# A fused hash-attention and channel-mix kernel on one Trainium2 core: a new preparation of the first pair, and new wanted times in its plan

## The chip, the cores and the metric

The kernel runs on one core of a Trainium2 chip. The metric is device time in microseconds (us) of one execution. The kernel before took 266.68 us as a median of three runs; with a further run beside the changed kernel 267.82 (266.32 to 269.33), and 268.2 to 268.6 on the three chips that the experiments used. All ratios below use fast runs only (a run is slow when it lies over 1.5% above the fastest of its kernel), and each kernel is compared with the kernel before in the same rounds on the same chip.

A ratio below is the mean time of one kernel's fast runs over that of the other's of the same rounds, so it is not quite the ratio of the medians that are quoted beside it. These medians are of all runs, slow ones included. Of the fast runs alone they are 270.20 for e_pool_hi, 269.97 for e_direct, 267.08 for e_old_start, 266.78 for e_old_w, 268.60 for e_jit1 and 260.43 for e_fix_w, 268.0 to 268.2 for the kernel before beside them, and as quoted for the others.

## The reference, cut to what matters

```python
# q, k, v: 4 batches x 8 heads x 768 x 64; proj: 64 x 6
q_bucket, k_bucket = ...          # six sign bits of q @ proj and k @ proj
mask   = q_bucket[..., :, None] == k_bucket[..., None, :]
scores = where(mask, q @ k.T / 8, -1e9);  attn = softmax(scores)
x      = (attn @ v), heads side by side    # 4 x 768 x 512
xk, xr = mu * x + (1 - mu) * (x one row earlier)
k = max(xk @ w_k, 0);  out = sigmoid(xr @ w_r) * ((k * k) @ w_v)
```

The 32 heads are worked in 16 pairs, four pairs to a batch. The channel mix ("moe" in the code) of a batch can start when its four pairs are done. So at the start TensorE has attention work only, and later it can fill holes with channel mix.

## The kernel before

Nothing in the program text says in which order operations run. Every operation is added to a plan with an engine, an estimated duration and a *wanted time*, mostly counted in pairs. The plan is a small simulation: whenever an engine is free, it takes the ready operation that was wanted first. The order that comes out is the program of each engine, and on the chip each engine executes its program strictly in that order.

```python
for e in free:                       # each engine that is free at plan time t
    while ready[e]:
        item = heapq.heappop(ready[e])          # smallest wanted time
        ...                                     # (cut: score and small PSUM buffers)
        if o.svc > 0.3 and dma_free - t > BACKLOG:
            skipped.append(item); ...           # a large load waits for the queue
            continue
        pick = o
        break
    ...
    free[e] = t + o.dur                         # the plan believes o.dur
```

To prepare a pair, q and k are split in a high half (`hi`) and the rest (`lo`), transposed (pairs 0 and 1 on TensorE, later ones by DMA), multiplied by the projection for the bucket bits, and the bits become six more rows of the transposed operands. For pair 0 this was done whole head by whole head; for pairs 1 and 2 GpSimd made `hi`.

```python
POOL_HI = (1, 2)
add("GQ", 0.6, -20.0, lambda e=e: nc.gpsimd.dma_start(out=pj[e * D : (e + 1) * D, :], in_=proj), ...)
...
def hi(side=side, nat=nat, nh=nh, hp=hp):
    (nc.gpsimd if hp else nc.vector).tensor_scalar(out=nh[:, :, 0:D], in0=nat..., scalar1=QS, ...)
add("POOL" if hp else "DVE", 0.8 if hp else DVE_C(768, 2), n - 1.95, hi, ...)   # n - 1.95 is the wanted time
...                                             # pair 0: six transposes, then one copy of 768 columns
for c in range(NSC):
    nc.tensor.transpose(ps[:, c * P : (c + 1) * P], nh[:, j * NSC + c, :], idh)
```

The softmax here doesn't subtract the row's maximum and nothing guards it: scores larger than these inputs give would overflow.

Of the kernel before, what the change touches and what calls it, by code (L numbers as in the profile page):

```python
# [20 lines left out]
BACKLOG = 1.5  # L21

# [5 lines left out]
class Plan:  # L28
# [44 lines left out]
    def schedule(self):  # L73
# [17 lines left out]
        t = 0.0  # L91
        dma_free = 0.0
        while len(order) < len(ops):
# [19 lines left out]
            for e in free:  # L113
# [4 lines left out]
                while ready[e]:  # L118
                    item = heapq.heappop(ready[e])
                    o = ops[item[1]]  # L120
                    if o.take is not None:
                        cls, name, moe = o.take
                        if not avail[cls] or (moe and moe_held[cls] >= self.slots[cls][1]):
                            skipped.append(item)
                            continue
                    if o.svc > 0.3 and dma_free - t > BACKLOG:
                        skipped.append(item)
                        heapq.heappush(events, (dma_free - BACKLOG, 3, o.i))
                        continue
                    pick = o  # L130
                    break
# [31 lines left out]
def kernel(  # L163
# [29 lines left out]
    NWARM = 8  # L193
    NPET = 1
    NUC = 4
    POOL_HI = (1, 2)
# [10 lines left out]
    def buf(shape, dt, name):  # L207
        return pool.tile(shape, dt, name=name, tag=name)
# [31 lines left out]
    pj = buf([P, NB], FP32, "pj")  # L240
# [16 lines left out]
    POOL2 = lambda n: 0.18 + 2.2 * n / 1000.0  # L257


    wz = buf([P, 512], BF16, "wz")  # L260
    add("DVE", 0.2, -20.0, lambda: nc.vector.memset(wz, 0.0), w=["wz"])
    for i in range(NWARM):
        add("PE", 0.43, -20.0 + 0.1 * i, lambda: nc.tensor.matmul(sm("warm"), wz[:, 0:P], wz, start=True, stop=True),
            r=["wz"], w=["warm"], take=("sm", "warm", 0) if i == 0 else None, give=["warm"] if i == NWARM - 1 else [])
    add("ACT", 1.3, -9.0, lambda: nc.scalar.activation(out=wz[:, 0:1], in_=wz[:, 1:2], func=AF.Exp), r=["wz"], w=["wz0"], name="table")
# [9 lines left out]
    for i in range(NXT):  # L275
        add("POOL", 0.1, -1.0 + i, lambda i=i: nc.gpsimd.memset(xt_t[i][:, 0:1], 0.0), w=[("xz", i)])
    for e in range(2):
        add("GQ", 0.6, -20.0, lambda e=e: nc.gpsimd.dma_start(out=pj[e * D : (e + 1) * D, :], in_=proj), w=[("pj", e)], svc=0.05)
    add("DVE", 0.08, -8.0, lambda: nc.vector.tensor_scalar(
        out=p1[:, 0:NB], in0=pj, scalar1=-1.0, scalar2=None, op0=ALU.mult),  # L280
        r=[("pj", 0), ("pj", 1)], w=["p1"])
    add("DVE", 0.08, -8.0, lambda: nc.vector.scalar_tensor_tensor(
        out=p2[:, 0:NB], in0=pj, scalar=-1.0, in1=p1[:, 0:NB], op0=ALU.mult, op1=ALU.subtract),
        r=[("pj", 0), ("pj", 1), "p1"], w=["p2"])
# [9 lines left out]
    wlist = [("k", c, 1) for c in range(NDC)] + [("r", 0, 2), ("r", 2, 2)] + [("v", c, 2) for c in range(0, NFC, 2)]  # L294
    for i, (which, c0, n) in enumerate(wlist):
# [6 lines left out]
        add("GQ", 0.7, (2.2 + 0.5 * i) if which == "k" else (3.5 + 0.35 * i), f_w, w=[("w" + which, c) for c in range(c0, c0 + n)], at=(22.0 + 5 * i) if which == "k" else (34.0 + 3.5 * i), svc=1.5)  # L302
# [4 lines left out]
    def add_load(n):  # L307
        b, t = divmod(n, NPB)
        s = n % NQ
        for side in "qk":  # L310
            if n == 0:
                for j in range(2):
                    def f(side=side, j=j):
                        eng = nc.sync if side == "q" else nc.scalar
                        eng.dma_start(out=side_nat[side][s][:, j, :],
                                      in_=SRC[side][b, 2 * t + j].rearrange("(p c) d -> p (c d)", c=NSC))
                    add("SP" if side == "q" else "ACT", 0.42, -10.0 + 0.1 * j, f,
                        w=[("nat", side, s, j)], svc=0.57)
            else:
# [3 lines left out]
                add("SP", 0.42, (n - 2.6) if n > 1 else -9.0, f, w=[("nat", side, s, j) for j in range(2)], svc=1.15)  # L323
# [4 lines left out]
        add("SP", 0.42, n - 2.1, fv, w=[("vn", n % NV)], svc=1.15)  # L328

    def add_v(n):  # L330
# [12 lines left out]
        if uc:  # L343
            add("POOL", 0.8, n - 0.3, f0, r=[("vn", s)], w=[("va", sa, 0), ("va", sa, 1)], name=f"va{n}")
# [10 lines left out]
        pr = n + 0.3 if uc else n - 0.6  # L355
# [13 lines left out]
        add("PE", 0.15, n - 0.1, f4, r=["ones", ("vs", ss)], w=[(nm,)], take=("sm", nm, 0), name=nm)  # L369
        for j in range(2):  # L370
# [5 lines left out]
            add("DVE", DVE_C(384), n + 0.0, f5, r=[(nm,), ("vn", s)], w=[("va", sa, j)], name=f"va{n}")  # L376
# [3 lines left out]
        add("DVE", DVE_C(1), n + 0.01, f6, r=[(nm,)], w=[("mc", sm_)], give=[nm])  # L380

    def add_prep(n):
        s, sh, sa, sx = n % NQ, n % NNH, n % NAQ, n % NBX
        for side in "qk":
# [14 lines left out]
            add("POOL" if hp else "DVE", 0.8 if hp else DVE_C(768, 2), n - 1.95, hi, r=rn, w=[("nhh", side, sh)], name=f"hi{n}")  # L399
            add("DVE", DVE_C(768), n - 1.95, lo, r=rn + [("nhh", side, sh)], w=[("nhl", side, sh)], name=f"lo{n}")  # L400
            if n <= NPET:
                for j in range(2):
# [7 lines left out]
                    add("PE", 6 * 0.056, n - 1.5, tp, r=["idh", ("nhh", side, sh), ("nhl", side, sh)], w=[(nm,)], take=("sm", nm, 0), name=nm)  # L410
                    add("DVE", DVE_C(768, 2), n - 1.45, ev, r=[(nm,)], w=[("a", side, sa, j), ("ab", side, sa, j)], give=[nm], name=f"tr{n}")
                continue
            add("SP", 1.5, n - 1.8, tr, r=[("nhh", side, sh), ("nhl", side, sh)],
                w=ax + [("ab", side, sa, j) for j in range(2)], svc=2.1, name=f"tr{n}")
        for h in range(2):
            nm = f"bits{n}_{h}"

            def f(nm=nm, h=h):
                ps = sm(nm)
                for w_, st in ((p1, True), (p2, False)):  # L420
                    for i in range(4):
# [4 lines left out]
            def g(nm=nm, h=h):  # L426
                nc.vector.tensor_scalar(  # L427
                    out=bx_t[sx][:, h * HALF : (h + 1) * HALF].bitcast(U16),
                    in0=sm(nm)[:, 0:HALF].bitcast(U16).rearrange("p (c e) -> p c e", e=2)[:, :, 1],
                    scalar1=0x8000, scalar2=0x5400, op0=ALU.bitwise_and, op1=ALU.bitwise_or)  # L430

            add("PE", 2 * MM(HALF) + 0.1, n - 1.2, f, r=["p1", "p2"] + [("a", side, sa, j) for side in "qk" for j in range(2)],
                w=[(nm,)], take=("sm", nm, 0), name=nm)
            add("DVE", DVE_C(HALF), n - 1.2, g, r=[(nm,)], w=[("bx", sx, h)], give=[nm], name=f"bx{n}")
        for i in (0, 1, 2, 3):
# [4 lines left out]
            add("SP", 0.7, n - 1.1 + 0.01 * i, row, r=[("bx", sx, 0), ("bx", sx, 1)], w=[("ab", side, sa, j)], svc=0.1, name=f"row{n}")  # L440

    def add_prep_first(n):
        s, sh, sa = n % NQ, n % NNH, n % NAQ
        for j in range(2):
            pr = -8.0 + 2.0 * j
            for side in "qk":
                nat, nh, a = side_nat[side][s], side_nh[side][sh], side_a[side][sa]
                nv = nat[:, j, :].rearrange("p (c d) -> p c d", d=D)
                def hi(nv=nv, nh=nh, j=j, side=side):
# [3 lines left out]
                    else:  # L453
                        nc.scalar.activation(out=o, in_=nv, func=AF.Copy, scale=QS)
                def lo(nv=nv, nh=nh, j=j):
# [3 lines left out]
                nm = f"t{side}{j}"  # L459
                def tp(nm=nm, nh=nh, j=j):  # L460
                    ps = sm(nm)[:, 0:HALF].bitcast(FP16)
                    for c in range(NSC):
                        nc.tensor.transpose(ps[:, c * P : (c + 1) * P], nh[:, j * NSC + c, :], idh)
                def ev(nm=nm, a=a, j=j, side=side):
                    i_ = sm(nm)[:, 0:HALF].bitcast(FP16)
                    if side == "q" and j == 0:
                        nc.vector.tensor_copy(a[:, j, :], i_)
                    else:
                        nc.scalar.copy(a[:, j, :], i_)
                if side == "q":  # L470
                    add("DVE", DVE_C(384, 2), pr, hi, r=[("nat", side, s, j)], w=[("fh", side, j)], name=f"hi{n}")
                else:
                    add("ACT", ACT_C(384), pr, hi, r=[("nat", side, s, j)], w=[("fh", side, j)], name=f"hi{n}")
                add("DVE", DVE_C(384), pr, lo, r=[("nat", side, s, j), ("fh", side, j)], w=[("fl", side, j)], name=f"lo{n}")
                add("PE", 6 * 0.09, pr, tp, r=["idh", ("fh", side, j), ("fl", side, j)], w=[(nm,)], take=("sm", nm, 0), name=nm)
                add("DVE" if side == "q" and j == 0 else "ACT", DVE_C(768, 2) if side == "q" and j == 0 else ACT_C(768), pr, ev,
                    r=[(nm,)], w=[("a", side, sa, j), ("ab", side, sa, j)], give=[nm], name="ev" + nm)
            for side in "qk":
                for h in range(2):
                    nm = f"b{side}{j}{h}"  # L480
                    a = side_a[side][sa]
                    def bits(nm=nm, a=a, j=j, h=h):
                        ps = sm(nm)
                        for w_, st in ((p1, True), (p2, False)):
                            nc.tensor.matmul(ps[D : D + 32, 0:HALF], w_, a[:, j, h * HALF : (h + 1) * HALF], start=st, stop=not st)
                    def be(nm=nm, a=a, j=j, h=h):
                        nc.vector.tensor_scalar(
                            out=a[D : D + NB, j, h * HALF : (h + 1) * HALF].bitcast(U16),
                            in0=sm(nm)[D : D + NB, 0:HALF].bitcast(U16).rearrange("p (c e) -> p c e", e=2)[:, :, 1],
                            scalar1=0x8000, scalar2=0x6C00 if (j == 0 and nm[1] == "q") else 0x5400, op0=ALU.bitwise_and, op1=ALU.bitwise_or)  # L490
                    add("PE", 2 * MM(HALF) + 0.1, pr + 0.1, bits, r=["p1", "p2", ("a", side, sa, j)], w=[(nm,)], take=("sm", nm, 0), name=nm)
                    def bs(nm=nm, a=a, j=j, h=h):
# [219 lines left out]
```

## Time and profile before

| | before |
|---|---|
| span of the profiled run | 266.3 us |
| TensorE busy, idle | 240.0, 26.3 us |
| idle before 26.3 us; 26.3 to 58.9; 58.9 to 125; after | 6.9; 7.4; 6.7; 5.3 us |
| exponential 1, 5, 10, 19, 37 starts at | 16.5, 21.4, 26.2, 39.6, 60.4 us |

Nine exponentials on ScalarE make one pair, so number 10 is the first of pair 1, 19 of pair 2, 37 of pair 4. They are good milestones, as they are the same work in each version. The prediction shows the totals and the first 16 us. From the timeline of TensorE these are three of the later holes; the figure in brackets is how long the engine stood before the group, and for what:

```profile
31.67 0.51 PE L573 MATMUL sm<-idb,ob 128*128 128x128 bf16 x6 [2.51 <-DVE ob L563]
...
83.01 0.22 PE L366 MATMUL sm<-vs,ones 128*128 128x128 bf16 x1 [2.05 <-POOL vs L353]
...
103.27 0.22 PE L366 MATMUL sm<-vs,ones 128*128 128x128 bf16 x1 [1.28 <-POOL vs L353]
```

Each is an operation that stands at the head of TensorE's program while its input is late. Nothing behind it can start, ready or not; how much was ready is not shown. That is the price of a fixed order when its estimates are wrong.

### The profile page before, as it was taken

To read this page: it belongs to the slowest core of one execution; us is meant where nothing else is said; L and a number is where in the kernel's file an instruction comes from. 1 tells how busy PE (TensorE), PEld (TensorE's weight loads), DVE (VectorE), ACT (ScalarE), POOL (GpSimd) and SP (SyncE) were. 2 spreads that over 40 slices of the span, in tenths; PEclk is the share of its full clock that TensorE was granted. 3 is DMA by queue.
4 is the path that set the end of the run, shared out by engine and by line. 5 is a ranking of instruction groups with operands and counts; after the bars stand their busy time and mean duration, and the time that the engine had idled before them with its cause. 6 is when DMAs were issued, how large, how long until landed. Compare 5 with 4: busy or idle time off the path is not lost.

```text
span 266.3 us, 6293 instructions
## 1 busy us (share of the span) xinstructions
PE 240.0 (90%) x2501; PEld 144.1 (54%) x2520; DVE 193.3 (73%) x386; ACT 185.9 (70%) x241; POOL 65.1 (24%) x103
## 2 busy tenths in 40 slices
PE   6597668878995897999999999999999999999994
PEld 2254446545663544565666665655666666556441
DVE  1799857699596998559898898858967655485322
ACT  3359579789687557688979887768798987437320
POOL 4799715064014204301140303020200000000000
PEclk9799999999999999999999999999999999999999
DMA  7953987769969667966949699768340011220132
GB/s 220 373 178 69 157 142 184 139 188 171 205 150 269 127 228 121 223 146 233 218 164 202 224 232 167 198 133 253 78 90 6 2 39 42 79 79 4 39 118 79
DMA packets 64525, 39.76 MB, mean 149 GB/s; under 512 B 46728, under 2 KB 60912, under 8 KB 64496
## 3 DMA queue, kind: packets, MB, share of 16 engines
q1 hardware_dynamic: 61936, 36.35, 54.0%
q0 software_dynamic: 2272, 2.63, 6.5%
q8 instruction: 19, 0.31, 0.5%
q10 hardware_dynamic: 288, 0.39, 0.5%
q14 instruction: 10, 0.08, 0.1%
HBM read 24.12 MB, written 6.29 MB: 114 GB/s over the span
## 4 chain that ended last, share of the span: by engine, by line
PE 69%; DVE 11%; DMA 8%; POOL 4%; ACT 3%; issue 3%; SPq 1%; DVEq 0%; POOLq 0%; ACTq 0%
PE sc L517 17%; PE sm L645 14%; PE sm L616 13%; PE sm L547 11%; PE sm L635 7%; DMA vn<-in_v_dram 4%; PE sm L423 4%; ACT pt L521 3%; DMA qn<-in_q_dram 2%; DVE kh L392 2%; PE sm L573 2%; DVE qh L392 2%; DMA ak<-bx 2%; POOL vt L347 1%; DVE qh L389 1%
## 5 line engine op out<-in xcount | busy, mean ns | idle before, releaser
L521 ACT ACTIVATE pt<-sc 128x1024 bf16<-128x1024 f32 x144 | 142.3, 1025 | 33.8 <-PE sc L517 33.2
L517 PE MATMUL sc<-aq,ak 128*128 128x512 f16 (+1 forms) x384 | 82.2, 325 | 6.8 <-ACT pt L521 5.3
L517 PEld LDWEIGHTS <-ak 128*128 128x128 f16 x384 | 34.3, 97 | 32.8 <-issue 11.2
L547 PEld LDWEIGHTS <-pt 128*128 128x128 bf16 x1152 | 42.9, 97 | 13.0 <-ACT pt L521 2.4
L616 PE MATMUL sm<-xk,wk 128*128 128x384 bf16 x256 | 47.6, 326 | 0.1
L547 PE MATMUL sm<-va,pt 128*128 128x65 bf16 x1152 | 45.5, 193 | 1.9 <-ACT pt L521 1.9
L645 PE MATMUL sm<-wv,k 128*128 128x512 bf16 x183 | 46.3, 379 | 0.7 <-issue 0.2
L620 ACT ACTIVATE kr<-sm 128x384 bf16<-128x384 f32 x64 | 30.7, 500 | 12.8 <-PE sm L616 11.9
L616 PEld LDWEIGHTS <-wk 128*128 128x128 bf16 x256 | 24.1, 98 | 15.0 <-issue 0.6
L347 POOL TENSOR_TENSOR vt<-vn 128x384 f32<-128x384 f32 x12 | 14.0, 1168 | 65.1 <-DMA vn<-in_v_dram 65.0
L652 DVE SCALAR_TENSOR_TENSOR os<-rs,sm 128x512 f32<-128x512 f32 x24 | 16.4, 682 | 17.9 <-PE sm L645 17.0
L623 DVE TENSOR_TENSOR k<-kr 128x384 bf16<-128x384 bf16 x64 | 22.9, 372 | 7.5 <-ACT kr L620 7.5
L638 ACT ACTIVATE rs<-sm 128x512 f32<-128x512 f32 x24 | 14.3, 598 | 19.9 <-PE sm L635 15.0
L583 POOL COPY xt<-xt 128x127 bf16<-128x127 bf16 x16 | 5.7, 359 | 89.8 <-DVE xt L579 76.4
L645 PEld LDWEIGHTS <-k 128*128 128x128 bf16 x192 | 18.0, 97 | 17.6 <-issue 0.6
L635 PE MATMUL sm<-wr,xr 128*128 128x512 bf16 x86 | 23.6, 379 | 0.5
L427 DVE TENSOR_SCALAR bx<-sm 128x384 uint16<-128x384 uint16 x30 | 15.5, 551 | 4.4 <-PE sm L423 3.3
L563 DVE TENSOR_TENSOR ob<-sm,rc 128x384 bf16<-128x384 f32 x32 | 17.8, 555 | 0.7
L392 DVE SCALAR_TENSOR_TENSOR kh<-kn,kh 128x768 f16<-128x768 f32 x15 | 16.3, 1085 | 0.8 <-POOL kh L389 0.5
L392 DVE SCALAR_TENSOR_TENSOR qh<-qn,qh 128x768 f16<-128x768 f32 x15 | 16.7, 1113 | 0.1
L599 DVE SCALAR_TENSOR_TENSOR xk<-df,muk,xt 128x768 bf16<-128x768 bf16 x16 | 16.2, 1015 | 0.3
L599 DVE SCALAR_TENSOR_TENSOR xr<-df,mur,xt 128x768 bf16<-128x768 bf16 x16 | 16.3, 1023 | 0.0
(79 smaller groups left out, 207.5 us busy)
## 6 DMA issues: line engine op xcount, KB each, us to landing
vn<-in_v_dram SPq DMA_DIRECT2D x16, 384.0 KB
out_dram<-os SPq DMA_DIRECT2D x24, 256.0 KB
qn<-in_q_dram SPq DMA_DIRECT2D x15, 384.0 KB
kn<-in_k_dram SPq DMA_DIRECT2D x15, 384.0 KB
wk<-in_moe_w_k_dram POOLq DMA_DIRECT2D x4, 256.0 KB, 4.4
wv<-in_moe_w_v_dram POOLq DMA_DIRECT2D x4, 256.0 KB, 7.7
wr<-in_moe_w_r_dram POOLq DMA_DIRECT2D x2, 256.0 KB, 4.2
aq<-bx SPq DMA_DIRECT2D x30, 9.0 KB
```

The lines of the kernel that those rows point to most:

```text
L347: nc.gpsimd.tensor_tensor(out=vt[:, :, :, 0:E], in0=src[:, :, 0:3, 0:E], in1=src[:, :, 3:6, 0:E], op=ALU.add)
L392: nc.vector.scalar_tensor_tensor(out=nh[:, :, D:P], in0=nat.rearrange("p j (c d) -> p (j c) d", d=D), scalar=QS, in1=nh[:, :, 0:D], op0=AL ...
L517: nc.tensor.matmul(ps[:, lo - s * STEP : hi - s * STEP], side_a["k"][sa][:, j, jc * P : (jc + 1) * P], side_a["q"][sa][:, j, q0 : q0 + hi ...
L521: nc.scalar.activation(out=pt_t[sp][:, s * STEP : (s + 1) * STEP], in_=sc_t[plan.slot[nm]], func=AF.Exp, bias=EBIAS, scale=ESC)
L547: nc.tensor.matmul(oo[:, ic * 65 : ic * 65 + 65], pt_t[sp][:, o : o + P], va_t[sa][:, j, jc, 0 : D + 1], start=(not uc and ic == 0 and jc ...
L563: nc.vector.tensor_tensor(out=ob_t[so][:, :, j * D : (j + 1) * D], in0=oo[:, :, 0:D], in1=rc_t[sr][:, 1, :].unsqueeze(2).to_broadcast([P, ...
L599: nc.vector.scalar_tensor_tensor(out=dst[smx], in0=df_t[sd], scalar=mu[:, t : t + 1], in1=x, op0=ALU.mult, op1=ALU.add)
L616: nc.tensor.matmul(ps[:, 0:HALF], wk_sb[:, d, fc * P : (fc + 1) * P], xk_t[mx[d]][:, h * HALF : (h + 1) * HALF], start=(d == 0), stop=(d = ...
L620: nc.scalar.activation(out=kr_t[sk], in_=sm(nm)[:, 0:HALF], func=AF.Relu, scale=0.5 ** 0.5)
L623: nc.vector.tensor_tensor(out=k2_t[s2][:, h * HALF : (h + 1) * HALF], in0=kr_t[sk], in1=kr_t[sk], op=ALU.mult)
L635: nc.tensor.matmul(sm(nr), xr_t[mx[d]][:, c * P : (c + 1) * P], wr_sb[:, d, :], start=(d == 0), stop=(d == NDC - 1))
L645: nc.tensor.matmul(sm(nv), k2_t[(b * NFC + fc) % NK2][:, c * P : (c + 1) * P], wv_sb[:, fc, :], start=(fc == 0), stop=(fc == NFC - 1))
```

## The change

The intent is an earlier start and a better order after it. The core of the diff:

```diff
-    NWARM = 8
+    NWARM = 7
-    POOL_HI = (1, 2)
+    POOL_HI = ()
-        add("GQ", 0.6, -20.0, lambda e=e: nc.gpsimd.dma_start(out=pj[...], in_=proj), ...)
+    add("ACT", 0.42, -20.0, lambda: nc.scalar.dma_start(out=pj, in_=proj), ..., at=0.75, svc=0.05)
...                                    (q and k of pair 0 now all on SP's queue, q and k in turn)
+            parts = [(0, 3), (3, 6)] if j == 0 else [(0, 6)]     # head 0 by halves
+                for e, (c0, c1) in enumerate(parts):             # transposes, copy, bits by part
...
+            if j == 1:
+                add_bits(n, (1,))       # head 1: bits on 64 partitions, rows by DMA
...
+                    if o.svc > 0.3 and o.prio > -9.0 and dma_free - t > BACKLOG:
+PR = {
+    'ldq': -2.811, 'ldv': -2.337, 'hi': -5.393, 'lo': -1.084, 'tr': -2.122, 'bits': -1.224, 'bx': -4.393, 'row': 4.034,
...
+    'tpe': -4.352, 'tev': -0.289, 'va_u': 2.059, 'vsum_u': -3.477, 'wk0': 38.237, 'wk1': 3.956, 'wr0': 54.984, 'wv0': 63.151,
+    'wv1': -2.812, 'p0b': -9.506,
+}
-            add(..., n - 1.95, hi, ...)
+            add(..., n + PR["hi"], hi, ...)          # and so for every operation
```

A few estimated durations in the plan were corrected too. No arithmetic changed.

## The prediction

> **What bounds the kernel now.** I read the page's totals first, then windows, the chain of waits in order of time, and the timelines of each engine over the first 60 us.
>
> ```profile
> span 266.3 us, 6293 instructions
> PE 240.0 (90%) x2501; PEld 144.1 (54%) x2520; DVE 193.3 (73%) x386; ACT 185.9 (70%) x241; POOL 65.1 (24%) x103
> PE   6597668878995897999999999999999999999994
> DVE  1799857699596998559898898858967655485322
> ACT  3359579789687557688979887768798987437320
> PEclk9799999999999999999999999999999999999999
> DMA  7953987769969667966949699768340011220132
> ```
>
> TensorE is busy 240.0 of 266.3 us, so it is idle 26.3 us, and the row of slices (6.66 us each) shows where: in the first sixteen. From slice 19 on it is full. Windows cut at the stage borders give the sizes (columns: stretch, length, then busy time of each engine, granted clock, DMA share, GB/s):
>
> ```profile
> 26.30:58.90 32.60, 25.23 (x365) 16.40 (x364) 24.80 (x43) 25.37 (x28) 13.46 (x21) 1.00 0.80 166
> 58.90:100.00 41.10, 35.88 (x392) 21.93 (x395) 34.27 (x70) 28.84 (x41) 9.92 (x16) 1.00 0.86 187
> 100.00:125.00 25.00, 23.50 (x271) 14.16 (x273) 18.16 (x36) 19.29 (x23) 5.23 (x7) 1.00 0.84 191
> 125.00:262.40 137.40, 135.97 (x1325) 81.49 (x1335) 96.88 (x208) 97.93 (x136) 16.13 (x27) 1.00 0.46 117
> ```
>
> TensorE idle per stretch is length minus the first busy figure: 7.4, 5.2, 1.5 and 1.4 us. After 262.4 it has nothing left, and the last eviction and store take 3.9 us. The remaining 26.3 - 7.4 - 5.2 - 1.5 - 1.4 - 3.9 = 6.9 us of idle lie before 26.3 us, and 3.8 us of what counts as busy there are eight warm-up matmuls. So two things bound the time: TensorE's work from about 100 us to the end, which this change does not shorten, and how soon the stages before it let TensorE run full. Any microsecond of early delay in which TensorE has nothing else to do goes to the end.
>
> The early stage runs on a chain that the timeline shows:
>
> ```profile
> 1.25 1.24 POOL L278 DMA_DIRECT2D pj<-in_proj_dram x2 [0.82 <-POOLq L696]
> 7.92 0.17 DVE L279 TENSOR_SCALAR p<-pj 128x6 f16<-128x6 f32 x1 [2.88 <-DMA pj<-in_proj_dram]
> 8.00 0.35 DVE L452 TENSOR_SCALAR qh<-qn 128x384 f16<-128x384 f32 x1
> 8.05 2.41 POOL L389 TENSOR_SCALAR qh<-qn 128x768 f16<-128x768 f32 x1 [3.85 <-DMA qn<-in_q_dram]
> 8.27 0.78 DVE L282 SCALAR_TENSOR_TENSOR p<-pj,p 128x6 f16<-128x6 f32 x1
> ...
> 10.54 2.29 POOL L389 TENSOR_SCALAR kh<-kn 128x768 f16<-128x768 f32 x1
> ...
> 12.87 0.96 DVE L392 SCALAR_TENSOR_TENSOR kh<-kn,kh 128x768 f16<-128x768 f32 x1 [0.53 <-POOL kh L389]
> ...
> 13.86 1.97 DVE L487 TENSOR_SCALAR aq<-sm 6x384 uint16<-6x384 uint16 x4
> ...
> 16.52 1.02 ACT L521 ACTIVATE pt<-sc 128x1024 bf16<-128x1024 f32 x1 [1.81 <-PE sc L517]
> ```
>
> VectorE stands still 2.88 us for the tiny projection, which was issued by GpSimd at 1.25 and landed at 7.9 behind the big loads. Its q part for the first head is queued behind that wait, although k had been converted on ScalarE from 3.93. Then pair 1's work, paced by GpSimd (2.41 and 2.29 us for what VectorE does in about 0.55), gets in front of the first pair's bucket rows (13.86). The first exponential is at 16.52.
>
> From there to 59.4 ScalarE does 36 exponentials of pairs 0 to 3. Four in a row take 3.77 us, 0.943 each, so 33.9 us of work in 42.9 us: 9.0 us of gaps. The largest is 2.82 us at 30.7, where TensorE's transposes of pair 0 waited for VectorE's ob (31.05), which stood behind pair 3's splitting. VectorE is busy 13.1 of 13.3 us between 13.3 and 26.6.
>
> **What the Trainium skill says.** "SBUF — State Buffer", section "Who interferes with whom": VectorE and GpSimd share a port pair, a VectorE operation with two SBUF inputs contends with a GpSimd operation that reads SBUF, and the loser blocks. The trace agrees: the VectorE split (L392) has median 957 ns but up to 1807, and the six-column L282 took 780 ns beside GpSimd's qh. "TensorE: Matmul & The Clock Gate", section "What's actually happening": after an idle window of about 3.4 us the clock halves. The trace shows a granted clock of 0.79 from 6.66 to 13.3 us; the first bucket matmuls (L485 on aq) took 434 ns against 329 later (L423, same columns). "DMA: Bandwidth & Descriptors", section "Issuing engines are not separate DMA queues": all issuers share the same 16 engines. So moving pj to ScalarE's queue helps because it is issued before the loads, not because the queue is another one; it took 3.9 to 5.9 us to land before.
>
> **The change part by part.**
> 1. *Projection first, on ScalarE's queue.* It is issued about 0.7 us instead of 1.25, by hardware generation, with only one large load ahead. The first large k loads, issued at 0.72, were in by 3.93, so I put pj at about 3.2 (estimate). The q chain can begin when q lands, about 4.2 instead of 8.0. The k loads move from ScalarE's queue to SP's, interleaved, some 0.45 us later by SP's issue times. Net about -3.5 us on the first chain.
> 2. *Halves.* Transpose, copy, bucket matmul and eviction go by 384 columns; scores need all q but only the half of k they use. The first k half need not wait for six transposes (0.85) and a 768-column copy (0.80): about -0.8. TensorE, no longer idle for 2.9 us there, should keep its full clock: six or so bucket matmuls before the scores at 0.1 less, -0.5.
> 3. *No pair-1 splitting on GpSimd.* VectorE gains 4 x 0.55 = 2.2 us of work; it loses two operations of about 0.5 us in part 4, and stretched splits (1.46 + 1.33 + 1.46 + 1.81 against 4 x 0.957 = 2.2 us over, not all of which vanish). About even in busy time. But pair 1 no longer waits 4.7 us for GpSimd (8.05 to 12.85), and the row evictions at 13.86 no longer wait behind it: about -1.5 on the first exponential.
>  First exponential: 16.5 - 3.5 - 0.8 - 0.5 - 1.5 = 10.2 us.
> 4. *Second head's rows by DMA.* Four evictions of 6 partitions become two of 64 (4 x 0.5 to 2 x 0.5), plus two row DMAs. Chain, all with durations from before: second-head split done about 8, transpose 0.8, copy 0.8, two bucket groups 1.9, eviction 0.5, two issues of 0.7: 13.4; a row then took 4.31 us at 34.53 in the chain of waits when queues were full, so 15.5 to 17.5. Four exponentials fill 10.2 to 14.0; the fifth, the first to need head 1, waits for about 16.5. It was at 21.4. So of the 6.3 us won at the first exponential about 4.9 survive; I count 4.5.
> 5. *New wanted times.* Splits' hi part first, lo later, xr two pairs later, k weights from 38 us rather than 22 to 37. This is aimed at VectorE's full stretch and at the DMA, busy 0.80 to 0.86 from 26 to 125 us. Of the 9.0 us of gaps between exponentials about 3 are needed anyway (score buffers changing hands, 0.15 to 0.3 between groups); of the 6 left I count 2.5 as won.
> 6. *Later gaps.* TensorE waited 3.3 us for the sums of v (L366), behind v loads of 4.3 and 5.3 us; these loads are wanted 0.24 pairs earlier. Of 6.7 us idle from 58.9 to 125 I count 1 as won.
>  Sum: -4.5 - 2.5 - 1 = -8.0; 266.7 - 8.0 = 258.7, rounded to 258.5.
>
> **The rivals.** (a) *The early gain is eaten by head 1's DMA or by the next bound.* The DMA share is 1.04 of its engines from 6.66 to 13.3 us, and rows go behind loads; VectorE is full to 35 us whatever comes first. For it: the row of 4.31 us. Against it: the new plan holds back v and pair-2 loads, and VectorE starts 4 us earlier. Then only 2 or 3 us come through: 264, within 2%. (b) *DMA becomes the bound.* The traffic is the same apart from two small rows, and 0.80 to 0.86 busy leaves at most a sixth. An attention pair every 9.5 us instead of 11 would need 0.80 x 11 / 9.5 = 0.93. Then parts 5 and 6 give nothing: 262. (c) *The plan fits better than I think.* Gaps between exponentials fall to 3 us and those from 58.9 on to 2: -4.5 - 6 - 4.7, hence 251.5. (d) *The plan fits worse*: each engine executes in program order, so one wrong guess blocks it, as ob did; bucket rows wanted four pairs late on the SP queue may stand behind transposes of 1.5 us. Then +3 against -4.5: 265.
>
> **Range and chances.** Rivals (a) and (b) set the upper end, 264; (c) nearly the lower, 252. The line for faster is 261.3, and lies 2.8 us above my value, about two thirds of an 8-in-10 half-width: 0.75 faster, 0.22 same, 0.03 slower, the last because nothing removed can come back with 5 us on top.
>
> **What would show it.** VectorE's wait for pj gone, and the q split at 4 to 5 us. First exponential at 9.5 to 11.5, fifth at 15.5 to 18 with a wait for a row DMA before it. No GpSimd qh. Last exponential of pair 3 at 51 to 54 instead of 59.4. First L616-type matmul near 60 instead of 68. TensorE idle about 18 us instead of 26.3, and from 125 us on still full. Wrong if the fifth exponential is later than 19, if TensorE's idle between 26 and 100 us does not fall, or if holes appear after 125 us.

## The result, and the profile after

The changed kernel took 259.5 us (258.52 to 261.46, four runs) against 267.82 before: ratio 0.9698, 95% interval 0.9607 to 0.979. A second set of six runs beside six fresh ones gave 0.9672 (0.963 to 0.9715). The prediction was 258.5 in 252 to 264, so it held. The path that it named after the first exponential did not, as the trace shows.

The totals and slices of the page after:

```profile
span 256.8 us, 6319 instructions
PE 239.3 (93%) x2519; PEld 143.5 (56%) x2519; DVE 195.1 (76%) x391; ACT 185.5 (72%) x242; POOL 57.9 (23%) x98
PE   6768898888999999999999989999999999999994
PEclk9998999999999999999999999999999999999999
```

TensorE's work is the same (239.3 us). Its idle time fell from 26.3 to 256.8 - 239.3 = 17.5 us, and the slices show that it is now full from slice 11 on but for one; before it was so from slice 17. The same stretches as in the prediction, the last one cut at 253, where TensorE ends:

```profile
0.00:26.30 26.30, 18.95 (x163) 9.84 (x164) 21.74 (x43) 15.30 (x21) 11.48 (x31) 0.94 0.79 224
...
26.30:58.90 32.60, 28.38 (x418) 18.23 (x415) 22.98 (x42) 28.63 (x30) 10.63 (x19) 1.00 0.95 178
58.90:100.00 41.10, 40.07 (x429) 24.75 (x429) 36.99 (x77) 32.17 (x46) 13.78 (x17) 1.00 0.95 189
100.00:125.00 25.00, 25.00 (x307) 15.49 (x303) 21.90 (x42) 20.64 (x24) 6.48 (x8) 1.00 0.81 206
125.00:253.00 128.00, 126.89 (x1218) 75.19 (x1216) 90.80 (x189) 88.73 (x125) 15.56 (x23) 1.00 0.44 116
```

Length minus the first busy figure gives idle of 7.4, 4.2, 1.0, 0.0 and 1.1 us, against 6.9, 7.4, 5.2, 1.5 and 1.4 before. The start, the visible subject of the change, holds no less idle time than before. The gain lies in the stages after it.

The start itself, from the timeline of all engines:

```profile
3.44 0.36 DVE L291 TENSOR_SCALAR p<-pj 64x6 f16<-64x6 f32 x2 [2.26 <-DMA pj<-in_proj_dram]
...
4.18 0.36 DVE L475 TENSOR_SCALAR qh<-qn 128x384 f16<-128x384 f32 x1
...
9.89 1.59 DVE L405 SCALAR_TENSOR_TENSOR qh<-qn,qh 128x768 f16<-128x768 f32 x1
10.54 1.96 ACT L557 ACTIVATE pt<-sc 128x1024 bf16<-128x1024 f32 x2
...
17.98 0.32 PE L443 MATMUL sm<-ak,p 128*32 128x384 f16 x1 [0.71 <-DVE ak L422]
...
20.20 2.90 ACT L557 ACTIVATE pt<-sc 128x1024 bf16<-128x1024 f32 x3 [3.86 <-PE sc L553]
```

The projection is in at 3.44 instead of 7.9, q is split from 4.18 instead of 8.0, and the first exponential starts at 10.54 instead of 16.52. But the fifth starts at 20.20, only 1.2 us earlier than before, after a wait of 3.86 us for scores. TensorE's program says why. In runs of the same source line it reads there:

```
... L553*3 L420*6 L443*16 L553*8 ...
    scores | last transposes, then all 16 bucket matmuls of pair 1 | scores of steps 4 and 5
```

The bucket matmuls of pair 1 (L443) stand ahead of the fifth scores, and they waited for VectorE's copies (L422), the last of which ended at 17.93. The chain of waits goes the same way, through those copies and 13 of those matmuls to the scores. VectorE was busy 6.22 of 6.64 us from 6.66 to 13.3 and 6.61 of 6.70 us from there to 20.0. So the start is bound by VectorE's program, and the tenth exponential moved only from 26.2 to 25.3. That program is not pair 1's work alone: three `hi` parts of pairs 2 and 3 (L402 at 12.93, 14.79 and 16.79, 2.0 us together) stand ahead of pair 1's last copy, because the new wanted time of `hi` is that early. The chain of waits runs through two of them (0.35 and 0.59 us).

The milestones of all kernels of this study, from their traces (start of the exponential in us; one profiled execution each, so a difference of a microsecond means little, as the two rows of the changed kernel show; the first exponential came at 10.2 to 12.0 in five traces of the same start, those of changed, second set, e_fix_w, e_fix_quiet and e_fix_both):

| | 1st | 5th | 10th | 19th | 37th | 144th |
|---|---|---|---|---|---|---|
| before | 16.5 | 21.4 | 26.2 | 39.6 | 60.4 | 228.0 |
| changed | 10.5 | 20.2 | 25.3 | 35.3 | 54.4 | 216.2 |
| changed, second set | 11.2 | 19.4 | 25.2 | 35.2 | 55.3 | 217.2 |
| e_old_times | 11.8 | 17.9 | 24.8 | 38.6 | 61.8 | 228.7 |
| e_old_start | 18.0 | 22.7 | 28.6 | 38.5 | 58.7 | 224.5 |
| e_pool_hi | 11.9 | 18.2 | 25.0 | 36.3 | 58.2 | 226.8 |
| e_direct (slow state) | 11.3 | 16.4 | 28.1 | 38.5 | 62.8 | 231.5 |
| e_old_w | 11.4 | 20.3 | 28.2 | 38.7 | 61.3 | 226.2 |
| e_jit1 | 11.9 | 19.5 | 25.5 | 35.8 | 57.7 | 228.1 |
| e_fix_hi | 12.1 | 19.9 | 26.0 | 39.1 | 60.1 | 222.2 |
| e_fix_w | 11.8 | 19.4 | 27.8 | 39.5 | 59.7 | 221.1 |
| e_fix_pj | 13.2 | 21.2 | 26.5 | 36.9 | 56.3 | 219.0 |
| e_fix_quiet | 12.0 | 18.5 | 24.0 | 34.4 | 53.3 | 217.4 |
| e_fix_both | 10.2 | 18.5 | 25.0 | 36.0 | 55.1 | 217.9 |

Of the 9.5 us between the two profiled spans (266.3 - 256.8), 0.9 us are there at the tenth exponential, 6.0 at the 37th, and 9.5 at the end. A lead in this table is not yet time won: at the 144th exponential it is 11.8 us, but 40.6 us of the changed kernel follow it, against 38.3 before.

### The profile page after: what moved, and what is told of

It is laid out like the page before. It is cut to its first block, busy times and chain, and to the rows that moved or that the text cites. A ratio compares the mean times of both kernels' runs of the same rounds, so it can differ in the third digit from the quotient of the medians.

```text
span 256.8 us, 6319 instructions
## 1 busy us (share of the span) xinstructions
PE 239.3 (93%) x2519; PEld 143.5 (56%) x2519; DVE 195.1 (76%) x391; ACT 185.5 (72%) x242; POOL 57.9 (23%) x98
## 4 chain that ended last, share of the span: by engine, by line
PE 63%; DMA 15%; DVE 10%; POOL 3%; SPq 3%; issue 2%; ACT 2%; POOLq 0%; DVEq 0%
PE sc L553 16%; PE sm L681 15%; PE sm L652 11%; PE sm L583 10%; DMA vn<-in_v_dram 8%; PE sm L671 7%; PE sm L443 4%; DMA qn<-in_q_dram 3%; DMA ak<-kh 2%; POOL vt L360 2%; DMA kn<-in_k_dram 2%; PE sm L609 2%; ACT pt L557 2%; SPq L334 1%; DVE xk L635 1%
## 5 line engine op out<-in xcount | busy, mean ns | idle before, releaser
L553 PE MATMUL sc<-aq,ak 128*128 128x512 f16 (+1 forms) x384 | 84.6, 329 | 4.5 <-ACT pt L557 4.5
L652 PE MATMUL sm<-xk,wk 128*128 128x384 bf16 x256 | 48.9, 326 | 0.2
L681 PE MATMUL sm<-wv,k 128*128 128x512 bf16 x192 | 47.8, 379 | 1.1 <-DVE ob L599 1.1
L583 PEld LDWEIGHTS <-pt 128*128 128x128 bf16 x1152 | 42.9, 97 | 9.0 <-issue 0.6
L360 POOL TENSOR_TENSOR vt<-vn 128x384 f32<-128x384 f32 x12 | 15.1, 1256 | 71.5 <-DMA vn<-in_v_dram 71.5
L659 DVE TENSOR_TENSOR k<-kr 128x384 bf16<-128x384 bf16 x64 | 23.8, 385 | 8.5 <-ACT kr L656 8.4
L681 PEld LDWEIGHTS <-k 128*128 128x128 bf16 x192 | 18.4, 98 | 19.5 <-issue 1.3
L688 DVE SCALAR_TENSOR_TENSOR os<-rs,sm 128x512 f32<-128x512 f32 x24 | 16.3, 684 | 16.5 <-PE sm L681 16.4
L671 PE MATMUL sm<-wr,xr 128*128 128x512 bf16 x96 | 24.6, 379 | 0.0
L619 POOL COPY xt<-xt 128x127 bf16<-128x127 bf16 x16 | 8.4, 525 | 69.1 <-DVE xt L615 64.4
L447 DVE TENSOR_SCALAR bx<-sm 128x384 uint16<-128x384 uint16 (+1 forms) x32 | 16.4, 549 | 3.3 <-PE sm L443 2.6
L405 DVE SCALAR_TENSOR_TENSOR kh<-kn,kh 128x768 f16<-128x768 f32 x15 | 18.3, 1219 | 0.1
L635 DVE SCALAR_TENSOR_TENSOR xk<-df,muk,xt 128x768 bf16<-128x768 bf16 x16 | 16.7, 1046 | 0.3
L443 PE MATMUL sm<-ak,p 128*32 128x384 f16 x124 | 14.4, 335 | 2.3 <-DVE ak L422 1.3
L635 DVE SCALAR_TENSOR_TENSOR xr<-df,mur,xt 128x768 bf16<-128x768 bf16 x16 | 16.1, 1018 | 0.0
```

The lines of the kernel that those rows point to most:

```text
L360: nc.gpsimd.tensor_tensor(out=vt[:, :, :, 0:E], in0=src[:, :, 0:3, 0:E], in1=src[:, :, 3:6, 0:E], op=ALU.add)
L405: nc.vector.scalar_tensor_tensor(out=nh[:, :, D:P], in0=nat.rearrange("p j (c d) -> p (j c) d", d=D), scalar=QS, in1=nh[:, :, 0:D], op0=AL ...
L443: nc.tensor.matmul(ps[32 * i : 32 * i + 32, 0:HALF], w_, a[:, i // 2, h * HALF : (h + 1) * HALF], start=st, stop=not st)
L553: nc.tensor.matmul(ps[:, lo - s * STEP : hi - s * STEP], side_a["k"][sa][:, j, jc * P : (jc + 1) * P], side_a["q"][sa][:, j, q0 : q0 + hi ...
L583: nc.tensor.matmul(oo[:, ic * 65 : ic * 65 + 65], pt_t[sp][:, o : o + P], va_t[sa][:, j, jc, 0 : D + 1], start=(not uc and ic == 0 and jc ...
L635: nc.vector.scalar_tensor_tensor(out=dst[smx], in0=df_t[sd], scalar=mu[:, t : t + 1], in1=x, op0=ALU.mult, op1=ALU.add)
```

## The experiments

There are two kinds. In the first kind a part is undone and the plan lays everything out anew, as the author of the change would do it. In the second kind (names with "fix") the order that the plan of the changed kernel gave is kept, and only the named operations are run on another engine or put at another place. All twelve kernels gave correct results.

### Start or times: e_old_times and e_old_start

```diff
 e_old_times: all of PR and the weights' load times set to the values before (hi -1.95, lo -1.95, row -1.1, ...); p0b -4.7,
              which puts head 1's bits where they were wanted before
 e_old_start: PR kept; NWARM = 8, POOL_HI = (1, 2), pj by GpSimd, k on ScalarE's queue, add_prep_first of before
```

> The new start (projection first, halves, rows by DMA, no GpSimd splitting) with the wanted times of the kernel before, the weights' load times too. Theory 1, the prediction's split: the start is worth 4.5 us and the times 3.5, so this is about 4.5 us under the kernel before (263 us). Theory 2, from the trace of after: of 6 us won at the first exponential only 1.0 is left at the tenth (25.3 against 26.3), the rest comes from the later stages, so this is only 1 to 2 us under before (265.5 to 266.5).

> The old start (whole first pair, projection by GpSimd, GpSimd splitting pairs 1 and 2) with all new wanted times. Theory 1: 3.5 us under before (264). Theory 2: 6 to 8 us under before (259.5 to 261), nearly as fast as the changed kernel; the first exponential back at about 16 us, TensorE's idle from 58.9 to 125 us still near 1 us.

Measured: e_old_times 266.78 us, ratio 0.9958 (0.9929 to 0.9987); e_old_start 267.45, ratio 0.9961 (0.9926 to 0.9996). Each alone, planned anew, gave 0.4%, some 1 us. Together they give 3%. Theory 1 fell for both. Theory 2 held for the start and fell for the times. The parts do not add up, and neither theory had reckoned with that. In e_old_times the 37th exponential is even later than before (61.8); in its trace TensorE waited 5.7 us in all, before that point, for the bucket rows of k to land by DMA.

### One part back: e_pool_hi and e_direct

```diff
 e_pool_hi:
-    POOL_HI = ()
+    POOL_HI = (1, 2)
 e_direct:
-                if j == 0:              # bits evicted straight into the operand
+                if True:                # for head 1 too, by VectorE
-            if j == 1:
-                add_bits(n, (1,))
```

> The changed kernel with the hi parts of pairs 1 and 2 back on GpSimd. Theory 1: pair 1 waits some 4.7 us for GpSimd as before, the tenth exponential moves back by 1 to 3 us and the time rises by 1 to 3. Rival: VectorE is full from 7 to 20 us, so taking 2.2 us off it balances the wait and the time stays within 1 us.

> The changed kernel with the second head's bucket rows of pair 0 written by VectorE in four evictions of 6 partitions, as before, not by two evictions and two DMAs. Theory of the prediction: the row DMA holds the fifth exponential back by about 2.5 us, so it comes earlier without it (17.5 or so instead of 20.2). Rival from the trace of after: the fifth waits because TensorE's program has pair 1's transposes and bucket matmuls, which wait for VectorE, ahead of it; then this changes the fifth by under 1 us or makes it later, as VectorE has 1 us more to do, and the total by under 1 us.

Measured: e_pool_hi 271.0 us, ratio 1.0115 (1.0034 to 1.0197); e_direct 271.43, ratio 1.0123 (1.0021 to 1.0224), its profile in the slow state. Both are *slower than the kernel before*, by about 1% on three fast runs each (by the record's line of 2% that is "same" and "unclear"), with all other parts of the change in place. In e_pool_hi the tenth exponential did not move (25.0) and the 19th came 1.0 us later, so most of the loss is not where the part acts, on pairs 1 and 2. In e_direct the fifth came at 16.4, but its plan also put the fifth scores ahead of pair 1's bucket matmuls, so this run does not separate the row DMA from the order, and on that question it is inconclusive. Its later milestones are from a profile in the slow state and are not read.

Other traces separate the two. In e_old_times and e_pool_hi head 1's rows go by DMA too, but pair 1's bucket matmuls are done by 17.0 and 16.8 us. There the fifth scores did wait for the row of k, 0.20 and 0.71 us, and the fifth exponential came at 17.9 and 18.2:

```profile
17.82 0.82 PE L553 MATMUL sc<-aq,ak 128*128 128x512 f16 x4 [0.71 <-DMA ak<-bx]
```

In the changed kernel the semaphores of the two row DMAs were complete at 16.8 and 17.6 us (from the packed trace), while the bucket matmuls ended at 19.2. So the rows came about as late as the prediction feared, and the order of TensorE's program cost about 1.5 us on top.

These four results suggested another theory: a change of any part makes a new plan, and the wanted times fit one plan only.

### No part changed at all: e_jit1

```diff
-    'ldq': -2.811, 'ldv': -2.337, 'hi': -5.393, ...
+    each value plus a random amount between -0.05 and 0.05
```

> The changed kernel with every wanted time moved by a random amount of at most 0.05 (of a pair), nothing else. Theory A: the parts of the change have their own worth and the plan is robust; the time stays within 1 us of the changed kernel (259 to 261). Theory B: undoing any part in the last four runs lost 3 to 4 per cent because the plan is laid out anew and the wanted times fit only the plan they were set for; then this moves the time by 2 to 8 us too (262 to 268).

Measured: 268.62 us over 20 runs, ratio 1.0025 (0.9997 to 1.0053). Theory B held, and more strongly than I had written: nothing of the gain is left, though every part of the change is there and no wanted time moved by more than a twentieth of a pair. The milestones agree to about a microsecond up to the 28th exponential (45.9 against 45.4), then the trace loses what it had. TensorE's idle time from 58.9 to 100 us is 41.10 - 35.19 = 5.9 us, against 1.0 in the changed kernel and 5.2 before:

```profile
58.90:100.00 41.10, 35.19 (x383) 21.36 (x380) 33.66 (x67) 26.59 (x38) 12.22 (x16) 0.96 0.80 187
```

On VectorE's timeline, between 74 and 85 us:

```profile
74.75 0.55 DVE L402 TENSOR_SCALAR qh<-qn 128x768 f16<-128x768 f32 x1
75.22 0.56 DVE L402 TENSOR_SCALAR kh<-kn 128x768 f16<-128x768 f32 x1
75.69 0.95 DVE L405 SCALAR_TENSOR_TENSOR qh<-qn,qh 128x768 f16<-128x768 f32 x1
...
79.42 1.35 DVE L402 TENSOR_SCALAR kh<-kn 128x768 f16<-128x768 f32 x1
80.69 1.05 DVE L659 TENSOR_TENSOR k<-kr 128x384 bf16<-128x384 bf16 x2
81.66 0.95 DVE L405 SCALAR_TENSOR_TENSOR qh<-qn,qh 128x768 f16<-128x768 f32 x1
```

The splits of two pairs (L402, L405) run with only two squares of the channel mix (L659) between them. The squares free the buffers that ScalarE's relu writes (ScalarE stood 1.65, 2.42 and 3.07 us for L659 from here to 88.7), and TensorE's next operations stand behind the relu:

```profile
81.82 1.30 PE L583 MATMUL sm<-va,pt 128*128 128x65 bf16 x36 [1.87 <-ACT kr L656]
...
89.23 0.48 PE L443 MATMUL sm<-aq,p 128*32 128x384 f16 x1 [2.40 <-ACT kr L656]
```

Before the second of these waits VectorE was on the inputs of the channel mix (L615 to L635, 84.97 to 88.30) and not on splits. So on this evidence, which is one random draw, the changed kernel's speed belongs to an order of operations and not to its parts or the rough position of its wanted times. That it is such collisions that cost the time is read from this trace and was not tested.

### The weights' times: e_old_w

```diff
-        add("GQ", 0.7, 2.5 + 0.3 * i, f_w, ..., at=W_AT[i], svc=1.5)
+        add("GQ", 0.7, <as before>, f_w, ..., at=(22.0 + 5 * i) if which == "k" else (34.0 + 3.5 * i), svc=1.5)
```

> The changed kernel with the weights loaded at the old wanted times (22 to 37 and on). Theory: in e_old_times and e_pool_hi TensorE waited 5.6 to 5.7 us for bucket row DMAs of k; with the weights' 2.6 MB in the way of pairs 1 to 3 these waits come back by 3 us or more and the time rises by 3 or more. Rival: the rows are held by the SP queue's own order, so the waits stay under 1 us and the time within 2 us.

Measured: 267.66 us, ratio 0.994 (0.9909 to 0.9971). The waits of TensorE for k's bucket rows came back (5.6 us in all, the longest 3.0), as the theory had it, and the tenth exponential moved to 28.2. But by the last run's lesson the total of 7 us could as well be the new plan's, so the same traffic was tried in the old order.

### The parts in a fixed order: e_fix_hi, e_fix_w, e_fix_pj

```diff
 e_fix_hi: (order of operations as in the changed kernel)
-                (nc.gpsimd if hp else nc.vector).tensor_scalar(out=nh[:, :, 0:D], ...
+                (nc.gpsimd if n in (1, 2) else nc.vector).tensor_scalar(out=nh[:, :, 0:D], ...
 e_fix_w: after plan.schedule() the four loads of w_k are taken out of the order and put back behind
          the second sum of v of pair 2 (one), pair 3 (two) and pair 4 (one)
 e_fix_pj:
-    lambda: nc.scalar.dma_start(out=pj, in_=proj)
+    lambda: nc.gpsimd.dma_start(out=pj, in_=proj)
```

> The changed kernel in its own order of operations, only the hi parts of pairs 1 and 2 run on GpSimd in the places that the plan gave them on VectorE. What GpSimd itself costs, without a new plan: in e_pool_hi part and plan were changed together (267 to 271). If the part is what counts, the tenth exponential is 3 us later or more and the time 3 us up or more; if the plan was, it stays within 2 us of the changed kernel.

> The changed kernel in its own order on every engine but GpSimd, where the four loads of w_k are issued at about 20, 30, 30 and 40 us, near their times in e_old_w, instead of 40 to 55. The weights' traffic alone, without a new plan. Traffic theory: TensorE waits for bucket rows again (3 us or more before 60 us), the tenth exponential comes at 27 to 28 as in e_old_w, and 2 us or more of the loss of e_old_w (7 us) appear. Rival: the loss of e_old_w was the new plan; then within 1 us of the changed kernel.

> The changed kernel in its own order on every engine, only the projection is loaded by GpSimd's queue instead of ScalarE's. The prediction's first part: it lands at 5 to 8 us instead of 3.4, VectorE waits for it ahead of q's splitting, the first exponential moves back by 2 to 4 us. Rival for the total: VectorE and the tenth exponential set the pace; if VectorE only shifts, the tenth moves back by as much and the time rises by 2 to 4 us; if VectorE has slack before 25 us the time rises by under 1 us.

Measured:

| | median us | ratio to before (95%) | changed kernel's ratio |
|---|---|---|---|
| e_fix_hi | 263.08 | 0.9798 (0.9714 to 0.9881) | 0.9698 and 0.9672, other chips |
| e_fix_w | 261.92 | 0.9741 (0.967 to 0.9811) | 0.9672, same rounds |
| e_fix_pj | 260.77 | 0.972 (0.9673 to 0.9766) | 0.9672, same rounds |

In a fixed order each part costs little when undone: 1.0 to 1.3% for `hi` on GpSimd, about 0.7% for early weights, about 0.5% for the late projection. The intervals overlap those of the changed kernel, so the totals alone prove little, but the milestones of the traces point the same way. (Against the kernel before, at the record's line of 2%, the first two are "unclear".) For e_fix_hi the time rose by about 3 us, as I had expected if the part counts, but not by the path: the tenth exponential (3 us later expected) was 0.8 later, and what came was a loss of about 5 us at the 37th. (Its profiled run was the slowest of its four, and those of e_fix_w and e_fix_pj were above their means too, so these milestones overstate the loss by 1 to 2 us.) For e_fix_w the traffic theory held in the trace:

```profile
27.06 1.16 PE L553 MATMUL sc<-aq,ak 128*128 128x512 f16 x4 [3.81 <-DMA ak<-bx]
```

One load of 256 KB was issued at 20.15, just ahead of pair 1's rows, and landed at 26.65; the three rows issued from 21.36 to 22.94 landed at 26.8 to 27.3. In the changed kernel, without that load, rows issued from 21.30 to 22.88 landed at 23.8 to 24.7. The scores of pair 1 stood 3.81 us for them. The 37th exponential was 4.3 us later than in the same rounds' changed kernel. Less than 2 us of it were left in the mean time, so the expected loss in the total was not quite reached. For e_fix_pj:

```profile
5.04 0.36 DVE L291 TENSOR_SCALAR p<-pj 64x6 f16<-64x6 f32 x2 [3.86 <-DMA pj<-in_proj_dram]
```

The projection came 1.6 us later than at 3.44, and everything up to the 37th exponential moved by 1 to 3 us. The mean time rose by about 1.2 us, less than the 2 to 4 expected.

### A better kernel: e_fix_quiet and e_fix_both, and the changed kernel again

If VectorE's preparation of pair 1 sets the pace of the start, lightening it should gain.

```diff
 e_fix_quiet: GpSimd's work on v of pair 0 moved behind pair 1's splits in the order, with a small copy that makes it wait:
+                nc.gpsimd.tensor_copy(tb[:, 1:2], side_nh["k"][1][:, 0, D : D + 1])
 e_fix_both: the same, and pair 1's two k-side copies on ScalarE:
-                        nc.vector.tensor_copy(a[:, j, :], sm(nm)[:, 0:HALF].bitcast(FP16))
+                        if side == "k": nc.scalar.copy(...)
+                        else: nc.vector.tensor_copy(...)
```

> The changed kernel in its own order, but GpSimd's work on v of pair 0 held back by one small copy until VectorE has split pair 1. Port theory: the two splits that took 1.59 and 1.60 us beside GpSimd fall to 0.96, pair 1's transposes, copies and rows come 1.0 to 1.3 us sooner, the tenth exponential is at 24.0 to 24.5 instead of 25.3 and the time 0.5 to 1.5 us lower. Rival: the splits are long for another reason and stay so; or the tenth exponential does not move as the v work then slows the copies; time within 0.5 us.

> The changed kernel in its own order, GpSimd's v work of pair 0 held back as in e_fix_quiet, and pair 1's two k-side copies on ScalarE instead of VectorE. If VectorE's work for pair 1 is what sets the tenth exponential, it comes at 22.5 to 23.5 instead of 24.0 (e_fix_quiet) and 25.3 (changed), and the time is 1 to 2 us under the changed kernel. Rival: what is won before the tenth exponential is taken back later, as in e_fix_quiet (1.3 us ahead at the tenth, 1.2 behind at the 144th); then within 1 us of the changed kernel.

> The changed kernel once more, for the comparison with the next run on the same chip. Expected ratio to the kernel before 0.97.

Measured: e_fix_quiet 258.99 us, ratio 0.9652 (0.9585 to 0.972). VectorE's timeline of that run:

```profile
10.14 0.95 DVE L405 SCALAR_TENSOR_TENSOR qh<-qn,qh 128x768 f16<-128x768 f32 x1
11.01 0.95 DVE L405 SCALAR_TENSOR_TENSOR kh<-kn,kh 128x768 f16<-128x768 f32 x1
```

The port theory held: the same two splits that took 1.59 and 1.60 us in the changed kernel take 0.95 each with GpSimd quiet, and the tenth exponential comes at 24.0. But its lead at the 37th (1.1 and 2.0 us over the two traces of the changed kernel) was gone at the 144th (1.2 and 0.2 us behind), and the total is not clearly lower. e_fix_both, 259.09 us, ratio 0.9662 (0.9618 to 0.9706), stood beside the changed kernel with five rounds: 259.72, ratio 0.9672 (0.963 to 0.9715). Its rival held: the same within 0.5%, and its tenth exponential (25.0) missed the expectation; the two splits took 0.95 us there too, so a tenth at 24.0 does not follow from them alone. No run of this study is shown to beat the changed kernel.

One figure separates the two kinds of kernels: TensorE's idle time between 58.9 and 100 us, length minus busy time as above. It is 0.8 to 2.2 us in the two traces of the changed kernel and in all five that keep its order, and 4.1 to 8.5 us in the kernel before and in all six with a new plan.

## Why the prediction was right, and where it was not

The total was right (258.5 predicted, 259.5 measured), in part by luck. Its terms were mis-sized in opposite directions, and its assumption that the parts' gains simply add, whatever plan comes out, was wrong.

- *Parts 1 to 3, the first exponential.* Their sum held; the terms were not isolated. The projection landed at about 3.4 (3.2 predicted), q's split began at 4.18 (4.2), the first exponential came at 10.54 (10.2). That the last figure fits so well is partly luck. Part 2 counted on a full clock for the bucket matmuls. In this trace those of q took 326 ns (median), against 458 before; in nine other traces of the new start, the second set's among them, they took a mean of 518 to 522 ns, and there the first exponential came at 11.2 or later. (`PEclk` shows 1.00 in such stretches too, as time before the first clock record is counted as full.)
- *Part 4, "of the 6.3 us won at the first exponential about 4.9 survive; I count 4.5".* This step failed. The prediction itself named a fifth exponential after 19 us as the sign of being wrong; it came at 20.20 and in the second set at 19.4. At the fifth 1.2 us were left and at the tenth 0.9. The chain worked out for head 1 left out that TensorE's program held pair 1's bucket matmuls ahead of the fifth scores, and that VectorE, busy 12.83 of the 13.34 us from 6.66 to 20.0, had to prepare pair 1, and some of pairs 2 and 3, first. No wait of TensorE before the fifth exponential was put down to the row DMA. The rows themselves landed at 17.6 us, just past the 15.5 to 17.5 that the prediction gave them; the step that it left out, TensorE's order, then cost 1.5 us, and part of the fifth scores ran at half clock (halved from 18.25 us).
- *Part 5, the gaps between exponentials.* The prediction measured 9.0 us of gaps over the 36 exponentials from the first and counted 2.5 as won. Over all 36 none were: from the first start to the last end it took 44.0 us, against 42.9, as the gaps among the first nine grew. After them the gaps shrank. By milestones, exponentials 10 to 36 took 60.4 - 26.2 = 34.2 us before and 54.4 - 25.3 = 29.1 after, so 5.1 us were won.
- *Part 6, later gaps.* I counted 1 us. In the prediction's own terms, TensorE's idle from 58.9 to 125 us fell from 6.7 to 1.0, so 5.7 were won; that is the largest share of the gain. By milestones 9.5 - 6.0 = 3.5 us came after the 37th exponential. The waits for the sums of v that the prediction quoted (3.3 us) do not appear in the list of TensorE's waits any more.
- *The sum.* Predicted 4.5 + 2.5 + 1 = 8.0. Measured in the traces 0.9 + 5.1 + 3.5 = 9.5. It came out right because the loss in the start's term was made up by the two others. That is luck. By TensorE's idle time the account is -0.5 us before 26.3, then 3.2 to 58.9, 5.7 to 125 and 0.4 after, 8.8 in all, with 0.7 us less of work.
- *The other signs.* The last exponential of pair 3 ended at 54.5 us (51 to 54 expected; 55.4 in the second set), and the first matmul of the channel mix came at 63.4 (near 60 expected). TensorE's idle fell to 17.5 us (about 18 expected) and from 12.6 to 5.2 between 26 and 100 us, and after 125 us it stayed full. (From its row of slices the prediction read "full from slice 19"; the row says 17.)
- *The rivals.* (a) was right that VectorE's fullness eats the early gain, though not by a DMA. (b) did not bind: the DMA share rose to 0.95 from 26 to 100 us (0.93 was the prediction's figure), and yet TensorE's idle fell there. (c) was nearest for the later stages. (d) named the mechanism, "each engine executes in program order, so one wrong guess blocks it", but expected it to show in this plan. It shows in the neighbours: six kernels with a part or a number altered and a new plan ran at 0.994 to 1.012 of the time before.
- *What is shown and what is not.* Shown: of the gain of 3% at most 0.6% is left in each of the six kernels whose plan was laid out anew, one of them with every part in place (e_jit1, one draw), and a gain of 2.0 to 3.5% is there in the five that keep the order. Planned anew, neither the start nor the times alone brings it (e_old_times, e_old_start). Indicated, with overlapping intervals: in that order, GpSimd off the splits, late weights and the early projection contribute about 3, 2 and 1 us. Only supposed: that the wanted times, with their three decimals, came out of a search among many plans. How common such good orders are stays open, and so does what the halves, the row DMA and the full clock are worth in the fixed order, as none of them was undone there.

## What to carry to other kernels

When the order of instructions comes out of a planner, test a change of one part with the old order kept as well; a new plan cost 3% here with no part changed, and can hide or fake the part's worth. Follow an early gain through milestones of the same work to the end, as 6 us at the first exponential were 1 us at the tenth. And jitter tuned numbers by a little, more than once, before believing them: if the gain goes, keep the order itself, not the numbers.

## What the Trainium skill lacked or had wrong

- "GPSIMD Engine Reference", section 4.1 "Engine selection", calls GpSimd roughly line-rate for operations with one input. Here a multiplication by a constant of 128 x 768 from float32 to float16 took 2.13 to 2.44 us on GpSimd (e_fix_hi) and 0.55 us on VectorE (changed kernel).
- "SBUF — State Buffer", section "Who interferes with whom", was right that the two contend: with GpSimd quiet the two splits fell from 1.59 and 1.60 to 0.95 us. That the loser fully blocks fits less well: in the kernel before L282 took 0.78 us and ended at 9.05, while GpSimd's `hi` ran from 8.05 to 10.46 (times on GpSimd are rough). A worked example of what that does to an engine in a full stretch would help, as here 1.3 us less of VectorE's work left no clear gain in the total.
- "TensorE: Matmul & The Clock Gate", section "What's actually happening", ties the slow clock to an idle window of about 3.4 us. In the changed kernel the granted clock was halved from 18.25 to 21.66 us, and bucket matmuls went from 0.33 to 0.52 us. In the 3.41 us before, TensorE was busy for 1.70 us and never stood longer than 0.71; in the 3.41 us before those it was busy for 2.64 us, and the clock stayed full. So here a half-busy window was followed by the slow clock too; the section gives no share that is busy enough.
- "DMA: Bandwidth & Descriptors", section "Specifications", gives first-byte latencies of about 0.6 and 1 us for the two ways of issue. The 1.5 KB projection was used 2.7 us after ScalarE began to issue it (0.73 to 3.44), and landed 3.4 us after GpSimd did, with large loads around it. No figure there says what a small transfer costs behind a large one: in e_fix_w a row of 9 KB issued 2.0 us after a load of 256 KB took 4.8 us to land, and 1.9 us in the changed kernel without that load.
- No page says how much an in-order program that a planner laid out can vary: moving the wanted times by at most 0.05 of a pair, once, took the ratio to the kernel before from 0.97 to 1.0025.
